# A deep-and-cross network kernel: the first superblock's transposing load and W1 change places on the SyncE queue

## The chip, the cores and the metric

The kernel runs on one core of a Trainium2 chip. The metric is device time in microseconds (us); a lower value is better. The kernel before was run eight times: 128.59, 128.99, 129.03, 129.17, 129.41, 128.19, 129.28 and 130.51 us, with a median of 129.1 us.

## The reference

```python
B, F, D, L = 4096, 26, 16, 6
Din = min(F * D, 1024)            # 416
# x0: (4096, 416), ws: (6, 416, 416), bs: (6, 416), all bfloat16

def reference(x0, ws, bs):
    x = x0
    for l in range(ws.shape[0]):
        x = x0 * (x @ ws[l] + bs[l]) + x
    return x
```

Each layer multiplies the 4096 x 416 activations by a 416 x 416 matrix, adds a bias, multiplies elementwise by the first input x0 and adds the activations of the layer before. Written out, x after layer l is x0 * (1 + the sum of x_j @ ws[j] + bs[j] over all layers j up to l). The kernel uses this form.

## The kernel before, in words

**Tiling.** The kernel works with transposed activations: features lie on the 128 partitions and batch rows run along the free dimension. The 416 features are three chunks of 128 (`NC = 3`, together `DF = 384`) and a rest of 32 (`DR`), called the tail. The 4096 rows are cut into `NS = 4` superblocks of `SB = 1024` rows, each of two halves of `H = 512` or four groups of `G = 256`. A step n is one layer of one superblock; there are 24, superblock after superblock and within it layer after layer (L308 to L421). The last one is done with rows on the partitions, ready for the store (L423 to L491).

**One step on TensorE (PE).** PSUM keeps the running sum over the layers, so nothing is added back by hand. A step consists of:

- `chunk(0..2, 0)`: 36 matmuls for half 0 (L255 by way of `tile_mm`, each 128 deep and 32 wide, four side by side). Each waits for the eviction of its input of the step before (`s_xa`, L341), and in superblock 0 the first waits for the layer's weights (`s_w[l]`, L360).
- the row matmuls, the part of the product that comes from the 32 tail features (L383 and L399). They use the small weights `wt_sb` and `wc_sb`. They wait for the tail of the step before (`s_sw`, L374) and for its last eviction (`s_xb`, L369); in step 0 for `x0t_sb` (`s_te`) and the small weights (`s_wt`, `s_wtp`, `s_wc`, L378 to L393). Their end is announced by `s_ti` (L410). VectorE (DVE) may then evict half 0, and SyncE waits for it before it issues later weights.
- 12 matmuls of 256 columns for the tail's 32 output features, for all four row groups (L415), announced by `s_to`.
- `chunk(0..2, 1)`: 36 matmuls for half 1 (L421), announced one chunk at a time by `s_mb`.

**The other engines.** DVE evicts six 128 x 512 tiles in each step, computing (PSUM + bias sum) * x0 (L527). The tail has a path of its own: ScalarE (ACT) reads it from PSUM (L585) after `s_to`, GpSimd (POOL) multiplies it by x0 (L232), and ACT copies it to neighbouring lanes (L556), which gives `s_sw` for the next step's row matmuls.

**The input of superblock 0.** Row blocks 0 to 5 (rows 0 to 767) are loaded as they lie into `xin_sb` (L135 to L137), are transposed by PE (L302, and L281 for blocks 4 and 5) and are copied into `x0T_sb` by DVE and ACT. The tail features of rows 768 to 1023 come in `xtl_sb` (L139). The 384 main features of rows 768 to 1023 come by a transposing load straight into `x0T_sb[:, :, 768:1024]` (L157, semaphore `s_x0T[0]`). PE waits for that in step 0 alone, at L412, after the row matmuls and before the tail matmuls, which are the first to read these rows, in their fourth group:

```python
ins.then_inc(s_ti, 1)                      # L410
if n == 0:
    pe.wait_ge(s_x0T[0], 16)               # L412
for k in range(NC):
    for g in range(4):
        ins = tile_mm(... src[:, k, off + g * G:off + (g + 1) * G], g, False)
```

**The queues around the change.** The SyncE queue (SP) issues by hand, in this order: the biases (L134), row blocks 0 and 1 (L135), row blocks 4 and 5 (L136), the transposing load L157, the main weights W1 of layer 1 (L163 with l = 1, 312 KB, `s_w[1]`), and four loads of the tail weights `wt_sb` of layers 1 to 5 (L125 through L165, `s_wt[1]`). Nothing among these waits. Then SP waits for `s_ti` before it issues W2 and the rest (L159). The ACT queue issues row blocks 2 and 3 (L137), W0 (L138), `xtl_sb` (L139) and two small `wt_sb` loads for layer 0 (L548, issued by L125, `s_wt[0]`). The POOL queue issues two `wt_sb` loads for layer 0 (`s_wtp`) and four `wc_sb` loads (L196), of which the first two are layer 0's (`s_wc[0]`).

Of the kernel before, what the change touches and what calls it, by code (L numbers as in the profile page):

```python
# [11 lines left out]
def bass_standalone__dcn_v2_cross__recsys_kernel(  # L12
# [9 lines left out]
    DF = 128 * NC  # L22
    DR = D - DF
    assert DR == 32
    SB = 1024
# [7 lines left out]
    with ExitStack() as es:  # L33
        def sb(name, shape, dt=BF16):
            return es.enter_context(nc.sbuf_tensor(name, shape, dt))
# [7 lines left out]
        x0T_sb = sb("x0T_sb", [128, NC, B])  # L43
# [20 lines left out]
        def sem(name):  # L64
            return es.enter_context(nc.semaphore(name))
# [8 lines left out]
        s_x0T = [sem("s_x0T%d" % i) for i in range(NS)]  # L74
# [16 lines left out]
        def wmain(l):  # L91
            return ws[l, 0:DF, :].rearrange("(k p) n -> p k n", p=128)
# [12 lines left out]
        def lane(g):  # L105
            return slice(32 * g, 32 * g + 32)
# [9 lines left out]
        def store(eng, a, n, by_pool):  # L116
            eng.wait_ge(s_o, a + n - by_pool)
            if by_pool:
                eng.wait_ge(s_oP, by_pool)
            assert a % 2 == 0 and n == 2  # L120
            eng.dma_start(out_w[:, (j0 + a) // 2, :, :], o_sb[:, j0 + a:j0 + a + n, :]).then_inc(s_out, 16)

        def load_wt(eng, g, a, b, done):
            n0, n1 = ((0, 256), (256, DF))[g % 2]
            eng.dma_start(  # L125
                wt_sb[lane(g), a:b, 0:n1 - n0], ws[a:b, DF:D, n0:n1].rearrange("l p n -> p l n")
            ).then_inc(done, 16)
# [19 lines left out]
        @block.sync  # L147
        def _(sp):
            def load_rows(s):
                sp.dma_start_transpose(  # L150
                    x4_sb[:, s - 1:s, :], x0[s * SB:(s + 1) * SB, D - 128:D]
                ).then_inc(s_x4[s - 1], 16)
                sp.dma_start_transpose(
                    x0T_sb[:, :, s * SB:(s + 1) * SB], x0[s * SB:(s + 1) * SB, 0:DF]
                ).then_inc(s_x0T[s], 16)

            sp.dma_start_transpose(x0T_sb[:, :, 768:SB], x0[768:SB, 0:DF]).then_inc(s_x0T[0], 16)  # L157
            for l in range(1, L):
                if l > 1:  # L159
                    sp.wait_ge(s_ti, (1, 2, 2, 2)[l - 2])  # L160
                if l == L - 1:
                    load_rows(1)
                sp.dma_start(w_sb[:, l, :, :], wmain(l)).then_inc(s_w[l], 16)  # L163
                if l == 1:
                    for g in range(4):  # L165
                        load_wt(sp, g, 1, L, s_wt[1])
            for s in range(NS - 1):
                n = (s + 1) * L
                sp.wait_ge(s_xa, NC * n)
                sp.wait_ge(s_xb, NC * n)  # L170
                for c in range(NC):
                    sp.dma_start_transpose(
                        o_sb[:, s * JS:(s + 1) * JS, c * 128:(c + 1) * 128], xo_sb[:, s, c, :]
                    ).then_inc(s_oT, 16)
                sp.wait_ge(s_xt, n)
                sp.dma_start_transpose(ot_sb[:, s, :, :], xot_sb[:, s, :]).then_inc(s_ot, 16)
                if s < NS - 2:
                    load_rows(s + 2)
                if s == 0:
                    for g in range(4):  # L180
                        sp.dma_start(wl_sb[lane(g), :], ws[L - 1, DF:D, :]).then_inc(s_wl, 16)
                if s == 1:
                    sp.dma_start(x0n_sb[:, :, :].rearrange("p (g r) d -> p g r d", r=2), x0_w[:, j0 // 2:, :, :]).then_inc(s_x0n, 16)
                sp.wait_ge(s_oT, 16 * NC * (s + 1))
                sp.wait_ge(s_otc, s + 1)
                sp.dma_start(
                    out_v[:, s * JS:(s + 1) * JS, :], o_sb[:, s * JS:(s + 1) * JS, :]
                ).then_inc(s_out, 16)
            store(sp, 0, 2, 0)
            store(sp, 4, 2, 2)  # L190
# [458 lines left out]
```

## Time and profile before

| what | value |
|---|---|
| median of 8 runs | 129.1 us |
| the profiled execution's own time | 128.59 us |
| its span, first to last instruction | 127.3 us |
| PE busy | 123.1 us, 97% of the span |
| DVE busy | 99.8 us, 78% |
| ACT busy | 67.6 us, 53% |
| POOL busy | 24.1 us, 19% |
| granted TensorE clock | 9 tenths or more in all 40 slices; 1.0 for the core |

The page of the profile describes one execution. PE is the engine of the matmuls and PEld is its weight load, which runs beside it. "Idle before" is the time an engine stood still ahead of an instruction, with the instruction or the transfer that ended the wait. For a DMA the profile gives the time of issue and the time from there to landing, when its semaphore is complete; "SPq", "ACTq" and "POOLq" are the queues of the engines that issue. All stage times below count from the start of the span.

### The profile page before, as it was taken

Reading aid. Unit: us, or ns where it says so; the run is one execution under the profiler, and the core shown is the slowest. Engines: PE = TensorE matmul, PEld = TensorE weight load, DVE = VectorE, ACT = ScalarE, POOL = GpSimd, SP = SyncE. Lnnn points to the kernel's source line nnn. Section 1 sums busy time; section 2 is a strip of 40 time slices with the busy share of each in tenths; the row PEclk is TensorE's granted clock in tenths of the full one; section 3 lists DMA queues with packets and bytes.
Section 4 is the critical chain, followed back from the end, with each engine's and each line's share of the span. In section 5 each row is a group of like instructions: output and inputs, shape, how many; then the busy total and the mean of one; then the engine's idle time right before and its main releaser. Section 6 shows DMA issues by size and latency. Waiting matters only on the chain.

```text
span 127.3 us, 5318 instructions
## 1 busy us (share of the span) xinstructions
PE 123.1 (97%) x2410; PEld 62.2 (49%) x2410; DVE 99.8 (78%) x154; ACT 67.6 (53%) x146; POOL 24.1 (19%) x44
## 2 busy tenths in 40 slices
PE   7799999999999999999999999999999999999991
PEld 5554444445445445445445445444444444454660
DVE  2339779779779789788797797797797797797973
ACT  0627357476735555574743563574762564566830
POOL 7512102102012023022022022022021020220450
PEclk9999999999999999999999999999999999999999
DMA  3983299400009969720006769960007820430006
GB/s 104 278 194 106 47 224 244 122 5 0 5 3 128 153 109 226 218 83 5 0 5 128 145 113 233 324 205 0 0 5 46 176 56 0 160 113 5 0 28 245
DMA packets 32577, 13.49 MB, mean 106 GB/s; under 512 B 24870, under 2 KB 32556, under 8 KB 32556
## 3 DMA queue, kind: packets, MB, share of 16 engines
q1 hardware_dynamic: 31036, 12.12, 45.0%
q10 hardware_dynamic: 1328, 0.99, 2.5%
q8 instruction: 19, 0.31, 1.1%
q0 software_dynamic: 192, 0.06, 0.2%
q14 instruction: 2, 0.02, 0.1%
HBM read 3.86 MB, written 3.41 MB: 57 GB/s over the span
## 4 chain that ended last, share of the span: by engine, by line
PE 94%; DMA 3%; DVE 0%; ACTq 0%; issue 0%
PE ps L255 81%; PE ps L383 10%; DMA w_sb<-in_ws_dram 3%; PE ps L439 2%; PE ps L454 1%; DVE o_sb L540 0%; PE ps L478 0%; ACTq L137 0%; PE ps L399 0%; PE ps L484 0%
## 5 line engine op out<-in xcount | busy, mean ns | idle before, releaser
L527 DVE SCALAR_TENSOR_TENSOR xT_sb<-ps,cb_sb,x0T_sb 128x512 bf16<-128x512 f32 x120 | 81.0, 743 | 16.4 <-PE ps L383 16.3
L255 PE MATMUL ps<-xT_sb,w_sb 128*32 128x512 bf16 (+1 forms) x1596 | 84.2, 364 | 0.0
L255 PEld LDWEIGHTS ps<-xT_sb,w_sb 128*32 128x32 bf16 x1596 | 40.9, 97 | 37.2 <-issue 4.0
L556 ACT ACTIVATE xt_sb<-xt_sb 32x256 bf16<-32x256 bf16 x76 | 31.5, 414 | 15.7 <-POOL xt_sb L232 15.1
L585 ACT ACTIVATE t_sb<-ps,cb_sb 64x256 f32<-64x256 f32 x46 | 21.6, 469 | 31.1 <-PE ps L255 30.8
L232 POOL TENSOR_TENSOR xt_sb<-t_sb,x0t_sb 128x256 bf16<-128x256 f32 x20 | 13.5, 673 | 81.4 <-ACT t_sb L585 81.4
L255 PE MATMUL ps<-x0T_sb,w_sb 128*32 128x512 bf16 (+1 forms) x336 | 18.5, 364 | 0.8 <-DMA w_sb<-in_ws_dram 0.8
L527 DVE SCALAR_TENSOR_TENSOR xo_sb<-ps,cb_sb,x0T_sb 128x512 bf16<-128x512 f32 x18 | 12.1, 744 | 2.5 <-PE ps L383 2.5
L255 PEld LDWEIGHTS ps<-x0T_sb,w_sb 128*32 128x32 bf16 x336 | 8.5, 97 | 8.3 <-DMA w_sb<-in_ws_dram 0.9
L383 PE MATMUL ps<-xt_sb,wt_sb 32*128 32x512 bf16 x76 | 11.5, 379 | 0.0
L604 ACT ACTIVATE x0t_sb<-x_sb 32x512 bf16<-32x512 bf16 x12 | 7.5, 626 | 0.3
L399 PE MATMUL ps<-xt_sb,wt_sb 32*128 32x512 bf16 x38 | 7.4, 385 | 0.0
L383 PE MATMUL ps<-xt_sb,wc_sb 32*128 32x256 bf16 x76 | 7.3, 268 | 0.0
L383 PEld LDWEIGHTS ps<-xt_sb,wt_sb 32*128 32x128 bf16 x76 | 2.2, 92 | 8.1 <-DVE xT_sb L527 8.1
L383 PEld LDWEIGHTS ps<-xt_sb,wc_sb 32*128 32x128 bf16 x76 | 3.8, 93 | 2.2
L232 POOL TENSOR_TENSOR xot_sb<-t_sb,x0t_sb 128x256 bf16<-128x256 f32 x3 | 2.0, 675 | 12.6 <-ACT t_sb L585 12.6
L540 DVE SCALAR_TENSOR_TENSOR o_sb<-ps,x0n_sb 128x416 bf16<-128x416 f32 x6 | 3.3, 586 | 1.0 <-PE ps L484 0.9
L560 ACT ACTIVATE xo_sb<-ps,cq_sb 128x512 bf16<-128x512 f32 x5 | 3.3, 685 | 1.1 <-PE ps L383 1.1
L551 ACT ACT_TABLE_LOAD x1 | 1.3, 1283 | 3.6 <-issue 3.6
L130 PE MATMUL ps<-const-bfloat16-1.0 128*32 128x256 bf16 x40 | 2.3, 418 | 0.8 <-PEq L634 0.8
L439 PE MATMUL ps<-w_sb,xT_sb 128*128 128x416 bf16 x12 | 2.8, 340 | 0.0
L507 DVE CAST x0T_sb<-ps 128x256 bf16<-128x256 f32 x2 | 0.8, 420 | 2.5 <-PE ps L255 2.5
(52 smaller groups left out, 41.2 us busy)
## 6 DMA issues: line engine op xcount, KB each, us to landing
out_dram<-o_sb SPq DMA_DIRECT2D x3, 832.0 KB, 4.8
w_sb<-in_ws_dram SPq DMA_DIRECT2D x5, 312.0 KB, 4.6
x0n_sb<-in_x_dram SPq DMA_DIRECT2D x1, 832.0 KB, 5.5
xin_sb<-in_x_dram SPq DMA_DIRECT2D x2, 208.0 KB, 3.7
out_dram<-o_sb SPq DMA_DIRECT2D x2, 208.0 KB, 2.0
out_dram<-o_sb ACTq DMA_DIRECT2D x2, 208.0 KB, 2.0
w_sb<-in_ws_dram ACTq DMA_DIRECT2D x1, 312.0 KB, 4.3
xin_sb<-in_x_dram ACTq DMA_DIRECT2D x1, 208.0 KB, 2.7
```

Source lines behind the costliest of these rows:

```text
L130: nc.tensor.matmul(ps[lane(q % 4), 7, 0:256], lhsT=CONST[:, 0:32], rhs=CONST, start=True, stop=True, skip_group_check=True, tile_position= ...
L232: pool.tensor_tensor(out=dst, in0=t32_sb[:, n % 2, :], in1=x0t_sb[:, s, 0:G], op=ALU.mult).then_inc(s_xt, 1)
L255: return pe.matmul(dst, lhsT=lhsT, rhs=rhs, start=start, stop=True, skip_group_check=True, tile_position=(0, 32 * q),)
L383: return pe.matmul(dst, lhsT=lhsT, rhs=srct[lane(g), cols], start=l == 0 and start, stop=True, skip_group_check=True, tile_position=(32 * ...
L399: pe.matmul(ps[:, NC * h + 2, :], lhsT=wt_sb[lane(g), l, 0:128], rhs=srct[lane(g), :].rearrange("p (b r) -> p b r", b=2)[:, ::-1, :], star ...
L439: pe.matmul(ps[:, NAT_BANKS[t], 0:D], lhsT=xT_sb[:, (L - 1) % 2, k, rows], rhs=w_sb[:, L - 1, k, :], start=False, stop=True, skip_group_ch ...
L527: dve.scalar_tensor_tensor(out=dst, in0=ps[:, NC * half + c, :], scalar=cb_sb[:, c, l:l + 1], in1=x0T_sb[:, c, o:o + H], op0=ALU.add, op1= ...
L540: dve.scalar_tensor_tensor(out=o_sb[:, j0 + t, :], in0=ps[:, NAT_BANKS[t], 0:D], scalar=1.0, in1=x0n_sb[:, t, :], op0=ALU.add, op1=ALU.mul ...
L556: ins = act.activation(out=buf[lane(g), G:2 * G], in_=buf[lane(g ^ 1), 0:G], func=ACTF.Copy)
L560: act.activation(out=xo_sb[:, NS - 1, c, half * H:(half + 1) * H], in_=ps[:, NC * half + c, :], func=ACTF.Identity, bias=cq_sb[:, c:c + 1] ...
L585: ins = act.activation(out=t32_sb[HALVES[h], n % 2, :], in_=tail(h), func=ACTF.Identity, bias=cb_sb[HALVES[h], NC, l:l + 1],)
L604: ins = act.activation(out=x0t_sb[lane(g), s + 1, :].rearrange("p (b n) -> p b n", b=2), in_=src[:, ::-1, :] if g % 2 else src, func=ACTF. ...
```

## The change

The transposing load of rows 768 to 1023 is issued after W1 rather than ahead of it, still ahead of the four `wt_sb` loads. No other instruction changes, on any engine. SP's list has the same 31 entries, two of them exchanged.

```diff
-            sp.dma_start_transpose(x0T_sb[:, :, 768:SB], x0[768:SB, 0:DF]).then_inc(s_x0T[0], 16)
             for l in range(1, L):
                 if l > 1:
                     sp.wait_ge(s_ti, (1, 2, 2, 2)[l - 2])
...
                 sp.dma_start(w_sb[:, l, :, :], wmain(l)).then_inc(s_w[l], 16)
                 if l == 1:
+                    sp.dma_start_transpose(x0T_sb[:, :, 768:SB], x0[768:SB, 0:DF]).then_inc(s_x0T[0], 16)
                     for g in range(4):
                         load_wt(sp, g, 1, L, s_wt[1])
```

## The prediction

> **What bounds the kernel now.** I read the page first, for the chain of work that ended last. It is PE from end to end, apart from the start:
>
> ```profile
> PE 94%; DMA 3%; DVE 0%; ACTq 0%; issue 0%
> PE ps L255 81%; PE ps L383 10%; DMA w_sb<-in_ws_dram 3%; PE ps L439 2%; PE ps L454 1%; DVE o_sb L540 0%; PE ps L478 0%; ACTq L137 0%; PE ps L399 0%; PE ps L484 0%
> ```
>
> Any microsecond by which PE is late in step 0 therefore counts, unless something behind it absorbs it. Next I read the table of waits in the first 9.5 us, for the transfers that anybody waits for:
>
> ```profile
> PEld ps L255 <- DMA w_sb<-in_ws_dram: 0.9, 1, 0.9
> PE ps L255 <- DMA w_sb<-in_ws_dram: 0.8, 1, 0.8
> PEld ps L383 <- DVE x0T_sb L507: 0.5, 1, 0.5
> PEld ps L255 <- DMA bsa_sb<-in_bs_dram: 0.4, 1, 0.4
> PEld ps L255 <- issue: 0.2, 1, 0.2
> ```
>
> The transfers waited for are the biases and one weight load, W0, whose wait ends at 5.60. No row names the transposing load, W1 or the small weights. The two loads that change places are both hidden today, so the question is how well. The timeline gives the issues (start, duration, engine, line), and the list of DMA issues, asked for narrow windows, the landings (last column: us from issue to landing):
>
> ```profile
> 2.21 1.28 SPq L157 DMA_TRANSPOSE x0T_sb<-in_x_dram  x1
> 2.33 1.21 ACTq L125 DMA_DIRECT2D wt_sb<-in_ws_dram  x2
> 3.55 0.58 SPq L163 DMA_DIRECT2D w_sb<-in_ws_dram  x1
> 4.16 1.92 SPq L125 DMA_DIRECT2D wt_sb<-in_ws_dram  x4
> ```
>
> ```profile
> x0T_sb<-in_x_dram SPq DMA_TRANSPOSE x1, 5.4
> w_sb<-in_ws_dram SPq DMA_DIRECT2D x1, 312.0 KB, 4.8
> wt_sb<-in_ws_dram ACTq DMA_DIRECT2D x1, 8.0 KB, 5.0
> ```
>
> The transposing load lands at 2.21 + 5.4 = 7.6, W1 at 3.55 + 4.8 = 8.3, and the later of ACT's two small loads (issued at 2.85) at 7.85. Who reads them, and when, is in PE's weight-load timeline, with ACT's tail copies beside it:
>
> ```profile
> 8.27 0.09 PEld L383 LDWEIGHTS ps<-x0t_sb,wt_sb 32*128 32x128 bf16 x1 [0.47 <-DVE x0T_sb L507]
> 8.57 0.09 PEld L383 LDWEIGHTS ps<-x0t_sb,wc_sb 32*128 32x128 bf16 x1
> 8.90 1.96 PEld L255 LDWEIGHTS ps<-x0T_sb,w_sb 128*32 128x32 bf16 x48 [0.21 <-issue]
> 10.97 1.83 PEld L255 LDWEIGHTS ps<-xT_sb,w_sb 128*32 128x32 bf16 x36
> 13.22 0.09 PEld L383 LDWEIGHTS ps<-xt_sb,wt_sb 32*128 32x128 bf16 x1 [0.42 <-DVE xT_sb L527]
> ...
> 11.27 1.69 ACT L556 ACTIVATE xt_sb<-xt_sb 32x256 bf16<-32x256 bf16 x4 [0.79 <-POOL xt_sb L232]
> ```
>
> The wait of L412 stands ahead of the group at 8.90. So the transposing load has 8.90 - 7.6 = 1.3 us to spare. W1's first reader starts at 10.97, so W1 has 10.97 - 8.3 = 2.7 us. ACT's small weights, read at 8.27, have 0.4 us, and POOL's wc_sb (second load issued at 3.33, 4.8 us to landing, 8.1), read at 8.57, have 0.5 us.
>
> **W1 comes earlier.** It is issued at 2.21 and may land about 1.3 us sooner. Nobody waited for it, so this is worth 0.
>
> **The transposing load comes later.** Its issue moves by W1's own issue time, 0.58 us, to 2.79. If issue alone set its landing, it would land at 8.2. That is the lower bound. But the engines have work at that time: the table by windows shows 325 and 344 GB/s from 3 to 5 us, and a DMA share near or over 1 up to 8 us, so a load's landing is set by the bytes ahead of it. W1 is 312 KB, 319,488 bytes. At the mean of these two rates, 335 GB/s, it takes 0.95 us; at the 207 GB/s of the stretch from 5 to 6, the lowest there, 1.54 us. The landing is then 7.6 + 0.95 = 8.55, or 9.15 as the upper bound of this working. I take 8.55, because W1 itself ran in such a stretch (241 and 300 GB/s from 6 to 8 us) and landed only 0.7 us after the transposing load. 8.55 lies ahead of 8.90, so PE is not held.
>
> **If it is late after all,** not every bit of it counts. When PE starts its tail matmuls d later, DVE is not held: it evicts half 0 from 9.12 for 2 us anyway, while half 1's first chunk, 24 matmuls after 8.90, is there by about 10.2 (84 matmuls take 4.33 us in the chain), and is needed at 11.1. What shifts by d is the tail path (ACT L585, POOL L232, ACT L556), which ends at 11.27 + 1.69 = 12.96. The next row matmuls start at 13.22, held by DVE's last eviction; PE's own weight loads were through at 12.80, the idle 0.42 before 13.22. So 0.26 us is absorbed and the rest passes 1:1 to the end. The landing that decides is 8.90 + 0.26 = 9.16. Even the bound of 9.15 costs nothing that shows.
>
> **The loads that now stand beside others.** SP's four wt_sb loads (L125) keep their place behind both, with the same bytes ahead of them; their first reader is the row group at 13.22, against a last landing near 10. SP's next wait is for s_ti; it was through with its issues at 6.1 and waits until 9.0. The small loads of ACT and POOL are the delicate ones: they meet W1 where they met the transposing load. [...] The row says 5.0 us from issue to landing for 8 KB, landing 0.25 us behind the transposing load that SP began to issue 0.64 us earlier. As measured, it stood behind SP's work. If it now stood behind both SP loads, it would land at 7.85 + 0.95 = 8.8, the row matmuls of 8.27 would be 0.53 us late, and nothing absorbs that, since DVE's evictions wait for them (0.67 us before 9.12). I take a value between, from the order of issue: the transposing load would now begin at 2.79, only 0.06 us ahead of this small load. ACT's first small load stands like that today (2.33, against 2.21) and lands after 4.8 us, at 7.1, 0.5 ahead of the transposing load. The second would then land at 8.55 - 0.5 = 8.05, under 8.27: cost 0, with both ends, 0 and 0.53, kept. POOL's second wc_sb load by the same upper end would land at 9.05 against 8.57, 0.48 late, in the same stall and not added to it.
>
> **Could it gain?** PE's start at 5.61 hangs on W0 (ACT queue, issued 1.27). If W1's packets disturbed W0 less than the transposing ones, the start could move up, but not ahead of ACT's second input copy by much: that ends at 5.52 and the second third of the matmuls needs it. Also xtl_sb lands only at 1.79 + 4.8 = 6.6, and its transposes start at 6.91. So the gain is below 0.3 us.
>
> The sum is 0 us in the likely case, against the profiled execution's own 128.59 us (span 127.3 and 1.3 around it). The runs' median lies 0.5 us above that execution, and I set the difference on the median: 129.1 + 0.0 = 129.1 us. Against a measurement, 0.5% (0.65 us) is about what can be told from no change.
>
> **Rivals.**
> 1. The small weights become the wait. Mechanism: ACT's and POOL's small loads fall behind both SP loads. For it speaks the 5.0 us for 8 KB, against it the order of issue. Price 0.53 us: 129.6 us. It decides from a landing of 8.27.
> 2. The slower one: the transposing load does not stream behind W1 but runs after it, and the wait of L412 becomes real. [...] the nearest row, W2 issued alone at 9.02, landed after 2.9 us. Taken as a full serial cost, by the row, the landing is 7.6 + 2.9 = 10.5, which is 10.5 - 9.16 = 1.3 us too late: 130.4 us. For it speaks that the transposing load of superblock 1 (L153) took 8.0 us to land, 3.6 after its 4.4 us of issue. Against it: W1 landed 0.7 us behind the transposing load, so these loads overlap. It decides from a landing of 9.16.
> 3. The change takes effect and nothing follows, because both stay hidden: the forecast.
> 4. W0 gains the 0.3 us: 128.8 us, which counts as no change too.
>
> **How the numbers follow.** Forecast 0.60 (129.1); small weights late 0.16 (129.6, mostly within 0.5%, 0.03 of it beyond); serial transposing load 0.14 (130.4); W0 earlier 0.06; a gain over 0.65 us that I cannot name 0.04. Faster 0.05, same 0.78, slower 0.17. The runs before scatter from 128.2 to 130.5, so their median is uncertain by a few tenths. The range starts at 128.6 and ends at 130.1, past the small-weights case at 129.6 and its higher price (a full 1.54 for W1: 7.85 + 1.54 - 8.27 = 1.1, 130.2), without the serial case's full price. The likeliest case's own range is 128.8 to 129.5.
>
> **What would show it.** Right: in the profile after, the group at 8.90 has "issue" ahead of it and not a DMA, the transposing load lands between 8.2 and 9.15, W1 near 7, and the steps from 13.2 on have the same times. The small-weights case would show as a DMA wait ahead of L383 near 8.3, the serial one as a wait for x0T_sb ahead of L255 after 9. The prediction is wrong if the landing passes 9.16 or if W0's wait moves by more than 0.3 us.

## The result and the profile after

The changed kernel's median is 129.3 us (20 runs), against 128.55 us for the kernel before (57 runs, the eight shown earlier among them). The ratio is 1.0051, with a 95% interval of 1.0032 to 1.0070, so the change costs about 0.65 us. The ratio leaves out the few executions of a slower state that both kernels fall into now and then. A second series gave 1.0054 (1.0033 to 1.0075). No change was forecast; the kernel became slower, and the prediction was wrong. That 129.3 lies only 0.2 us from the forecast 129.1 is luck: the median of the first eight runs, on which the forecast stood, was 0.55 us above that of all 57.

The profiled execution after took 128.84 us with a span of 127.6. Its chain of waits has a new link:

```profile
PE 91%; DMA 4%; ACTq 2%; DVE 0%; issue 0%
PE ps L255 79%; PE ps L383 10%; DMA wt_sb<-in_ws_dram 4%; PE ps L439 2%; PE ps L454 1%; DVE o_sb L540 0%; ACTq L139 0%; ACTq L138 0%; ACTq L125 0%; PE ps L478 0%; ACTq L137 0%; PE ps L399 0%; PE ps L484 0%
```

Where W0 stood (w_sb, 3%), there is now a load of the small tail weights (wt_sb, 4%) with ACT's queue behind it. The table of waits up to 9.8 us says the same:

```profile
PEld ps L383 <- DVE x0T_sb L507: 1.2, 1, 1.2
...
PE ps L383 <- DMA wt_sb<-in_ws_dram: 0.7, 1, 0.7
...
PEld ps L255 <- DMA w_sb<-in_ws_dram: 0.3, 1, 0.3
```

Before, the row matmuls (L383) waited for DVE's input copy alone; now PE waits another 0.7 us, for wt_sb. The weight load's 1.2 us, put down to DVE, is the same wait: DVE's copy had ended at 8.09. The issues and the landings of the two exchanged loads and of ACT's second small load:

```profile
2.22 0.47 SPq L162 DMA_DIRECT2D w_sb<-in_ws_dram  x1
2.32 0.96 ACTq L125 DMA_DIRECT2D wt_sb<-in_ws_dram  x2
2.73 1.28 SPq L164 DMA_TRANSPOSE x0T_sb<-in_x_dram  x1
```

```profile
w_sb<-in_ws_dram SPq DMA_DIRECT2D x1, 312.0 KB, 5.0
...
x0T_sb<-in_x_dram SPq DMA_TRANSPOSE x1, 6.1
...
wt_sb<-in_ws_dram ACTq DMA_DIRECT2D x1, 8.0 KB, 5.5
```

W1 lands at 7.3, the transposing load at 2.73 + 6.1 = 8.8, the small load (issued at 2.84) at 8.4. Their readers in the timeline:

```profile
8.59 0.09 PEld L383 LDWEIGHTS ps<-x0t_sb,wt_sb 32*128 32x128 bf16 x1 [1.15 <-DVE x0T_sb L507]
8.62 0.37 PE L383 MATMUL ps<-x0t_sb,wt_sb 32*128 32x512 bf16 x1 [0.69 <-DMA wt_sb<-in_ws_dram]
...
9.16 1.96 PEld L255 LDWEIGHTS ps<-x0T_sb,w_sb 128*32 128x32 bf16 x48 [0.21 <-issue]
...
13.49 0.09 PEld L383 LDWEIGHTS ps<-xt_sb,wt_sb 32*128 32x128 bf16 x1 [0.42 <-DVE xT_sb L527]
```

From 13.49 on every step has its old length; the whole loss lies in step 0. The profiles bear this out: time less the start of step 1's row matmuls is 115.3 or 115.4 us in all thirteen profiled executions of this document but e1's (128.59 - 13.22 before, 128.84 - 13.49 after). This execution was among the faster ones of the changed kernel. Another one (e10_after_third, 129.66 us) has all three late loads as gates, one after the other:

```profile
8.95 0.09 PEld L383 LDWEIGHTS ps<-x0t_sb,wt_sb 32*128 32x128 bf16 x1 [1.49 <-DVE x0T_sb L507]
9.43 0.09 PEld L383 LDWEIGHTS ps<-x0t_sb,wt_sb 32*128 32x128 bf16 x1 [0.35 <-issue]
9.89 1.96 PEld L255 LDWEIGHTS ps<-x0T_sb,w_sb 128*32 128x32 bf16 x48 [0.32 <-DMA x0T_sb<-in_x_dram]
14.22 0.09 PEld L383 LDWEIGHTS ps<-xt_sb,wt_sb 32*128 32x128 bf16 x1 [0.42 <-DVE xT_sb L527]
```

against a second profiled execution of the kernel before (e9_before_again, 128.16 us):

```profile
7.91 0.09 PEld L383 LDWEIGHTS ps<-x0t_sb,wt_sb 32*128 32x128 bf16 x1 [0.59 <-DVE x0T_sb L507]
8.48 1.96 PEld L255 LDWEIGHTS ps<-x0T_sb,w_sb 128*32 128x32 bf16 x48 [0.21 <-issue]
12.81 0.09 PEld L383 LDWEIGHTS ps<-xt_sb,wt_sb 32*128 32x128 bf16 x1 [0.42 <-DVE xT_sb L527]
```

In e10 ACT's second small load landed at 8.73, POOL's second wc_sb load at 9.32 and the transposing load at 9.85, each followed by the row that reads it. Step 1's row matmuls come 1.41 us later than in e9; the two times differ by 1.50.

The loads in all profiled executions with these two orders of the queue, in us. A landing is the moment when the load's semaphore is complete (issue plus the list's last column; here with the trace's second decimal). The packet columns come from the trace's packet records: ACT's small loads are the 64 packets of 256 bytes on ACT's queue, the transposing load is the first 768 such packets on SP's. The kernel of e12, told below, has the changed order and differs in what PE waits for.

| kernel | W0 lands | ACT's small loads: last packet ends | second one lands | POOL's second wc_sb load lands | transposing load: first packet | lands |
|---|---|---|---|---|---|---|
| before | 5.56 | 6.67 | 7.84 | 8.09 | 5.00 | 7.60 |
| e9, before again | 4.87 | 6.37 | 7.69 | 7.91 | 5.01 | 7.43 |
| after | 4.94 | 6.46 | 8.38 | 8.59 | 6.03 | 8.82 |
| e5, after again | 4.98 | 7.05 | 9.08 | 9.43 | 6.04 | 9.87 |
| e10, after, third | 4.94 | 6.93 | 8.73 | 9.32 | 6.08 | 9.85 |
| e12, changed order | 5.29 | 6.48 | 7.87 | 8.45 | 5.86 | 8.82 |

The packets of ACT's small loads are through at 6.4 to 7.1 in both kernels, before PE wants the weights. What is late is the landing: it follows the last packet by 1.2 and 1.3 us in the kernel before, and by 1.4 to 2.0 in the changed order.

### The profile page after: what moved, and what is told of

The parts are those of the page before. It is cut to its first block, busy times and chain, and to the rows that moved or that the text cites. A ratio compares the mean times of both kernels' runs of the same rounds, so it can differ in the third digit from the quotient of the medians.

```text
span 127.6 us, 5318 instructions
## 1 busy us (share of the span) xinstructions
PE 123.4 (97%) x2410; PEld 62.5 (49%) x2410; DVE 99.9 (78%) x154; ACT 67.6 (53%) x146; POOL 24.1 (19%) x44
## 2 busy tenths in 40 slices
DMA packets 32577, 13.49 MB, mean 106 GB/s; under 512 B 24870, under 2 KB 32556, under 8 KB 32556
## 4 chain that ended last, share of the span: by engine, by line
PE 91%; DMA 4%; ACTq 2%; DVE 0%; issue 0%
PE ps L255 79%; PE ps L383 10%; DMA wt_sb<-in_ws_dram 4%; PE ps L439 2%; PE ps L454 1%; DVE o_sb L540 0%; ACTq L139 0%; ACTq L138 0%; ACTq L125 0%; PE ps L478 0%; ACTq L137 0%; PE ps L399 0%; PE ps L484 0%
## 5 line engine op out<-in xcount | busy, mean ns | idle before, releaser
L255 PE MATMUL ps<-xT_sb,w_sb 128*32 128x512 bf16 (+1 forms) x1596 | 84.2, 364 | 0.0
L255 PEld LDWEIGHTS ps<-xT_sb,w_sb 128*32 128x32 bf16 x1596 | 40.9, 97 | 37.2 <-issue 4.0
L255 PE MATMUL ps<-x0T_sb,w_sb 128*32 128x512 bf16 (+1 forms) x336 | 18.6, 366 | 0.1
L255 PEld LDWEIGHTS ps<-x0T_sb,w_sb 128*32 128x32 bf16 x336 | 8.6, 97 | 7.8 <-issue 1.0
L383 PE MATMUL ps<-xt_sb,wt_sb 32*128 32x512 bf16 x76 | 11.5, 379 | 0.0
L383 PE MATMUL ps<-xt_sb,wc_sb 32*128 32x256 bf16 x76 | 7.3, 268 | 0.0
L383 PEld LDWEIGHTS ps<-xt_sb,wt_sb 32*128 32x128 bf16 x76 | 2.2, 92 | 8.1 <-DVE xT_sb L527 8.1
L383 PEld LDWEIGHTS ps<-xt_sb,wc_sb 32*128 32x128 bf16 x76 | 3.8, 93 | 2.2
L383 PE MATMUL ps<-x0t_sb,wt_sb 32*128 32x512 bf16 x16 | 2.4, 378 | 0.7 <-DMA wt_sb<-in_ws_dram 0.7
```

The costliest lines, as they stand in the source:

```text
L255: return pe.matmul(dst, lhsT=lhsT, rhs=rhs, start=start, stop=True, skip_group_check=True, tile_position=(0, 32 * q),)
L383: return pe.matmul(dst, lhsT=lhsT, rhs=srct[lane(g), cols], start=l == 0 and start, stop=True, skip_group_check=True, tile_position=(32 * ...
```

## The experiments

Theory: step 0's small weights, which ACT and POOL load, land late because they share the fate of the transposing load, which is now behind W1; their wait is the loss. Rival: the transposing load's own wait (L412) is the loss. Third: W1's traffic delays W0 and PE's start. Line numbers shift by a few with the edits: L257, for example, is L255 in another kernel.

**e1_w1_on_act.** W1 ahead of the small loads, but on ACT, with the transposing load where it was.

```diff
         nc.scalar.dma_start(xtl_sb[:, :, :], x0_v[:, 6:JS, DF:D]).then_inc(s_xtl0, 16)
+        nc.scalar.dma_start(w_sb[:, 1, :, :], wmain(1)).then_inc(s_w[1], 16)
...
-                sp.dma_start(w_sb[:, l, :, :], wmain(l)).then_inc(s_w[l], 16)
+                if l > 1:
+                    sp.dma_start(w_sb[:, l, :, :], wmain(l)).then_inc(s_w[l], 16)
```

> W1 is issued by ACT between xtl_sb and ACT's two small wt_sb loads; the transposing load is issued on SP where it was before the change, so it is not behind W1 in its queue, but the small loads are. Small-weights theory (the row matmuls of step 0 wait for small weights that land behind W1): slower than the kernel before by 0.4 to 1.0 us (about 129.2 from 128.55), a DMA wait ahead of L383, small weights landing at 8.3 or later, although the transposing load lands near 7.6. Transposing-load theory (the wait of L412 is what costs): the same as before, 128.55 within 0.25 us, no DMA wait ahead of L383. W0 theory (W1's traffic disturbs PE's start): PE's start later than 5.6.

Ratio 1.0189 (1.0127 to 1.0250), some 2.4 us, far above the 0.4 to 1.0 expected; it rests on three executions (130.52, 130.90 and 131.92). The profiled one had a granted clock of 0.987, so only the order of landings is read from it. The wait, and the landings of the transposing load (issued at 2.21) and of ACT's second small load (issued at 3.62):

```profile
PE ps L385 <- DMA wt_sb<-in_ws_dram: 2.5, 1, 2.5
```

```profile
x0T_sb<-in_x_dram SPq DMA_TRANSPOSE x1, 7.7
...
wt_sb<-in_ws_dram ACTq DMA_DIRECT2D x1, 8.0 KB, 7.3
```

The small load, behind both, lands at 10.9 and holds PE, as the theory has it. Against the expectation, the transposing load, issued ahead of W1 in time, is late as well (9.9), so this run does not separate the two theories. The edit did something else too: ACT, busy issuing W1, began its own work at 4.25 instead of 3.57, and PE's matmuls stood 0.4 us for ACT's input copy (L553).

**e2_small_ahead.** The changed kernel with the small loads ahead of W1: ACT's two go to SP, and POOL's first two wc_sb loads to ACT.

```diff
+            for g in (1, 3):
+                load_wt(sp, g, 0, 1, s_wt[0])
...
-            for i in range(2):
-                for g in (1, 3):
-                    load_wc(i, g)
+            for g in (1, 3):
+                load_wc(1, g)
...
+            act.wait_ge(s_zero, 1)
             for g in (1, 3):
-                load_wt(act, g, 0, 1, s_wt[0])
+                act.dma_start(
+                    wc_sb[lane(g), 0:1, 32 * g:32 * g + 32], ws[0:1, DF:D, DF:D].rearrange("l p n -> p l n")
+                ).then_inc(s_wc[0], 16)
```

> The changed kernel, but step 0's small weights stand ahead of W1: ACT's two wt_sb loads go to SP between row blocks 4-5 and W1, and POOL's first two wc_sb loads go to ACT in their place. The transposing load is then still behind W1 and is issued 0.9 us later than in the changed kernel. Small-weights theory: the row matmuls are not held any more (L383 follows DVE's cast by 0.2 us or less), and the time falls back to 128.6 to 128.8. Transposing-load theory: stays at 129.2 or more, with a DMA wait ahead of L255 at about 9.

Ratio 1.0001 (0.9982 to 1.0019): the loss is gone, although the transposing load is still behind W1. Small loads landed by 7.5, the transposing load at 8.5:

```profile
8.70 0.09 PEld L384 LDWEIGHTS ps<-x0t_sb,wt_sb 32*128 32x128 bf16 x1 [0.47 <-DVE x0T_sb L508]
9.33 1.96 PEld L256 LDWEIGHTS ps<-x0T_sb,w_sb 128*32 128x32 bf16 x48 [0.21 <-issue]
```

Neither row has a DMA ahead of it. That the row matmuls are as late as 8.70 has another cause, told in the last section. The small weights (7.5) would have been in time for e9's 7.91 as well; the transposing load, landing at 8.54, would just have been late for e9's 8.48. It also lands earlier here than in the changed kernel (8.82 to 9.87), so this run alone does not part the two waits; e12 does.

**e3_third_ahead.** 104 KB of W1 ahead instead of 312 KB.

```diff
-                sp.dma_start(w_sb[:, l, :, :], wmain(l)).then_inc(s_w[l], 16)
+                if l == 1:
+                    sp.dma_start(w_sb[:, 1, 0, :], ws[1, 0:128, :]).then_inc(s_w[1], 16)
+                else:
+                    sp.dma_start(w_sb[:, l, :, :], wmain(l)).then_inc(s_w[l], 16)
                 if l == 1:
                     sp.dma_start_transpose(x0T_sb[:, :, 768:SB], x0[768:SB, 0:DF]).then_inc(s_x0T[0], 16)
+                    sp.dma_start(w_sb[:, 1, 1:NC, :], wmain(1)[:, 1:NC, :]).then_inc(s_w[1], 16)
...
-                            pe.wait_ge(s_w[l], 16)
+                            pe.wait_ge(s_w[l], 32 if l == 1 else 16)
```

> Only the first third of W1 (104 KB) goes ahead of the transposing load, the other two thirds follow it. Small-weights theory: the small weights land about a third as late as in the changed kernel (0.3 us less slack than before, of 0.4), so a loss of 0 to 0.25 us: 128.55 to 128.8. Transposing-load theory: its landing moves by 0.3 to 0.4 us and nothing is lost, 128.55. A fixed cost per load put ahead (not bytes) would leave most of the 0.65 us.

Ratio 1.0017 (0.9994 to 1.0041), no loss that can be told from zero. The small load lands at 7.70, the transposing load at 8.21. This speaks for a cost that grows with the bytes put ahead and against a fixed cost per load, which would have left most of the 0.65 us; the interval reaches 0.5 us, so it is not excluded.

**e4_w1_w2_ahead.** 624 KB ahead.

```diff
-                sp.dma_start(w_sb[:, l, :, :], wmain(l)).then_inc(s_w[l], 16)
+                if l != 2:
+                    sp.dma_start(w_sb[:, l, :, :], wmain(l)).then_inc(s_w[l], 16)
                 if l == 1:
+                    sp.dma_start(w_sb[:, 2, :, :], wmain(2)).then_inc(s_w[2], 16)
                     sp.dma_start_transpose(x0T_sb[:, :, 768:SB], x0[768:SB, 0:DF]).then_inc(s_x0T[0], 16)
```

> W1 and W2 (624 KB) go ahead of the transposing load; W2 is not held for s_ti. Small-weights theory: ACT's small loads were issued between W1 and the transposing load in time; if they stand behind W2 too, L383 is late by a further 0.9 us and the time is about 130.2; if they stand ahead of W2 (issue order), L383 stays as in the changed kernel and the transposing load, landing near 9.7, holds L255 by 0.5 to 0.8 us: 129.6. Transposing-load theory: landing near 9.7, L383 not held by a DMA, L255 held, 129.8 to 130.2.

Ratio 1.0126 (1.0086 to 1.0165), 1.6 us, more than the branch that fits its landings had (129.6). The transposing load lands at 10.40 and is waited for; POOL's second wc_sb load (9.26) and xtl_sb (7.50) were waits too, so the total is not one load's. The small load, issued at 2.84 ahead of the transposing load (3.27), lands at 7.98, 0.6 us after its last packet, where the changed order has 1.4 to 2.0. This hints that the place beside the transposing load, more than the bytes of W1, makes it late.

**e5_after_again.** The changed kernel, unedited.

> The changed kernel once more, for the size of the loss and a second profile. Small-weights theory: again 0.4 to 0.8 us over the kernel before, the start of the row matmuls of step 0 (L383) again set by a DMA wait for small weights, landing after 8.3, whether PE started early or late. If in this profile L383 follows DVE's cast without such a wait, or L255 waits for the transposing load, the theory holds only for the first profile.

Ratio 1.0054 (1.0033 to 1.0075). L383 stood until 9.37 for wt_sb (1.1 us), and L415's group until 9.94, just after the transposing load's landing at 9.87. The two waits nearly coincide.

**e6_act_small_ahead.** Of e2's edit only one half: ACT's two loads are put on SP ahead of W1, and POOL's stay.

> The changed kernel with ACT's two wt_sb loads alone put on SP ahead of W1; POOL's wt_sb and wc_sb loads stay as they are. If ACT's loads alone cost the time: back to the kernel before within 0.2 us, no DMA wait at L383. If POOL's wc_sb loads (8.59 in the changed kernel's profile, read 0.3 us after the first row matmul) are the next gate: a wait for wc_sb remains and 0.2 to 0.5 us of the loss stay. The transposing load lands near 8.9 and must not be waited for under the small-weights theory.

Ratio 1.0018 (0.9999 to 1.0036): about two thirds of the loss goes with ACT's two 8 KB loads, and the rest can't be told from zero. POOL's second wc_sb load landed at 7.6 without having been moved; the transposing load is issued behind it here (3.65, it at 3.33). In the profile PE waits for the transposing load, which was not to be under the theory:

```profile
7.88 0.09 PEld L385 LDWEIGHTS ps<-x0t_sb,wt_sb 32*128 32x128 bf16 x1 [0.45 <-DVE x0T_sb L509]
8.96 1.96 PEld L257 LDWEIGHTS ps<-x0T_sb,w_sb 128*32 128x32 bf16 x48 [0.65 <-DMA x0T_sb<-in_x_dram]
13.29 0.09 PEld L385 LDWEIGHTS ps<-xt_sb,wt_sb 32*128 32x128 bf16 x1 [0.42 <-issue]
```

**e7_before_small_ahead.** e2's small loads in the kernel before, ahead of the transposing load: a candidate for beating both kernels.

> The kernel before (transposing load ahead of W1) with step 0's small weights ahead of both on SP and ACT, as in e2_small_ahead. In the kernel before they land 0.4 us ahead of their reader, so they cost nothing in the profile; if in other executions PE comes to them earlier, they may. Expected 128.4 to 128.7, the same as before or up to 0.2 us faster.

Ratio 1.0010 (0.9992 to 1.0028): no gain. With 7.2 to 7.4 for the small weights nothing waits for them, but nothing waited before either.

**e8_transposing_load_last.** W1, the four wt_sb loads, then the transposing load.

```diff
                 if l == 1:
-                    sp.dma_start_transpose(x0T_sb[:, :, 768:SB], x0[768:SB, 0:DF]).then_inc(s_x0T[0], 16)
                     for g in range(4):
                         load_wt(sp, g, 1, L, s_wt[1])
+                    sp.dma_start_transpose(x0T_sb[:, :, 768:SB], x0[768:SB, 0:DF]).then_inc(s_x0T[0], 16)
```

> W1, then SP's four wt_sb loads (240 KB), then the transposing load, which lands about 0.7 us later than in the changed kernel, near 9.5. Does a late transposing load pass 1:1 to the end, or are 0.26 us absorbed as the prediction had it? With the group at L415 due 0.57 us after the first row matmul's weight load: 1:1 theory: the next step's row matmuls come later by all of the wait; absorption theory: by the wait less 0.26 us. Small-weights theory for the total: the same loss at L383 or less (the small loads now have W1 and some of the wt_sb loads ahead), plus the L415 wait: 129.2 to 129.9.

Ratio 1.0120 (1.0078 to 1.0162), above the range expected. ACT's second small load, issued at 2.84 as ever, and the transposing load, issued at 4.71:

```profile
wt_sb<-in_ws_dram ACTq DMA_DIRECT2D x1, 8.0 KB, 4.4
```

```profile
x0T_sb<-in_x_dram SPq DMA_TRANSPOSE x1, 5.3
```

The small load lands at 7.3, with W1 ahead of it and 80 KB of wt_sb issued beside it: earlier than in the kernel before. It lands 0.6 us after its last packet, as in e4. In this one execution W1 alone does not make it late, which points at the transposing load beside it. And the transposing load is now the wait:

```profile
8.68 0.09 PEld L383 LDWEIGHTS ps<-x0t_sb,wt_sb 32*128 32x128 bf16 x1 [0.47 <-DVE x0T_sb L507]
...
10.05 1.96 PEld L255 LDWEIGHTS ps<-x0T_sb,w_sb 128*32 128x32 bf16 x48 [0.87 <-DMA x0T_sb<-in_x_dram]
14.37 0.09 PEld L383 LDWEIGHTS ps<-xt_sb,wt_sb 32*128 32x128 bf16 x1 [0.42 <-issue]
```

**e9_before_again, e10_after_third, e11_small_ahead_again.** One profiled execution each, of the kernel before, the changed one and e2.

> The kernel before, one more look, for the scatter of its landings. Both theories: L383 follows DVE's cast by 0.6 us with no DMA wait; ACT's second small load lands at 7.6 to 8.1, the transposing load at 7.4 to 7.9, W1 after it. If the landings of the kernel before scatter as widely as those of the changed kernel (8.8 and 9.9 for the transposing load), the difference between the two is partly chance.

> The changed kernel, a third look. If the small loads share the fate of the transposing load they are issued beside: they land 0.4 to 0.8 us ahead of it, at 8.2 or later, and L383 waits for them; the transposing load lands at 8.7 to 9.9 and is due at about the same time, so that each of the two waits hides the other.

> Small weights ahead of W1 and of the transposing load, a second look. Small loads land by 7.5 and are not waited for; the transposing load, although issued 0.9 us later than in the changed kernel, lands at 8.4 to 9.0. If it lands near 9.9 here too, the recovery of this kernel is not due to the small weights alone.

e9 and e10 are in the table above: in two executions of the kernel before the three late landings differ by at most 0.2 us, in four of the changed order by 1.0 to 1.2, and each one's earliest is later than the latest of the kernel before (for ACT's load by 0.03 us only). e11 has the small wt_sb load at 7.30, but ACT's wc_sb load at 8.07, later than the 7.5 expected and still in time, and the transposing load at 9.06, which L256 waited for until 9.17, about when it was due.

**e12_rows_not_waited.** The changed kernel with the wait of L412 taken away; step 0 computes with other rows in place of the late ones.

```diff
-                        o = off + half * H
+                        o = off + half * (256 if n == 0 else H)
...
-                    if n == 0:
-                        pe.wait_ge(s_x0T[0], 16)
...
-                                src[:, k, off + g * G:off + (g + 1) * G], g, False,
+                                src[:, k, off + (g - (n == 0 and g == 3)) * G:off + (g - (n == 0 and g == 3) + 1) * G], g, False,
...
+                        elif n == 0:
+                            dve.wait_ge(s_x0T[0], 16)
```

> The changed kernel, but step 0 doesn't read the rows of the transposing load on PE: its fourth tail group and its half 1 read columns 512 to 767 and 256 to 767 of x0T_sb instead, and the wait for the transposing load stands on DVE ahead of half 1's evictions, at about 11. The work is the same, the values of these rows are not. What is left of the loss is then the small weights' alone. Small-weights theory as first stated (they are the whole loss): 0.4 to 0.7 us over the kernel before. If the two waits overlap, as in the third look at the changed kernel (row matmuls held to 8.95 and 9.43, the group at L415 to 9.89): 0.2 to 0.1 us less than the changed kernel's loss, so 0.4 to 0.6 us. If the transposing load is the larger part: under 0.25 us.

Ratio 1.0046 (1.0028 to 1.0064). Most of the loss, 0.6 of some 0.7 us, is there without any wait of PE for the transposing load; the interval (0.4 to 0.8 us) leaves room for all of it. Its profile is of the fastest of these executions (128.59 us), and there POOL's wc_sb load (8.45), not ACT's (7.87), is what PE stands for, 0.2 us beyond the 0.28 between the same two rows in e6:

```profile
8.09 0.09 PEld L383 LDWEIGHTS ps<-x0t_sb,wt_sb 32*128 32x128 bf16 x1 [0.48 <-DVE x0T_sb L505]
8.56 0.09 PEld L383 LDWEIGHTS ps<-x0t_sb,wt_sb 32*128 32x128 bf16 x1 [0.34 <-DVE x0T_sb L505]
8.91 1.96 PEld L255 LDWEIGHTS ps<-x0T_sb,w_sb 128*32 128x32 bf16 x48 [0.21 <-issue]
```

With e2 (1.0001) and e6 (1.0018) from the other side, the small weights' wait, ACT's and POOL's, is shown as the main loss. The transposing load's own wait mostly hides behind it (0.0 to 0.1 us in after, e5 and e10); the 0.2% that e6 has left fits it, but is not clear of zero.

## Why the prediction was wrong, point by point

- **What bounds the kernel; W1's worth.** Right. PE carries the chain, and W1's earlier landing (7.3 to 8.0 against 8.2 and 8.3, first read after 11) gained nothing.
- **The transposing load's landing.** Taken as 8.55, with 9.15 as the upper bound. Measured 8.82, 9.87 and 9.85. The term of 0.95 us for W1's 319,488 bytes, an estimate from the 335 GB/s of before, was too small for the landing: against 7.60 and 7.43 before, W1 ahead costs 1.2 us at the least and 2.4 at the most. It was right for the start, for the first transposing packet moved by about 1 us, from 5.0 to between 5.9 and 6.1. The rest came after that: the packets take 1.4 to 2.1 us from first to last (1.3 and 1.6 before), and the landing follows the last by 1.4 to 1.8 (1.0 and 1.1). The table by windows of e10, then of e9 (PEclk, DMA share and GB/s are the last three columns):

```profile
6.00:7.00 1.00, 1.00 (x37) 0.50 (x29) 0.00 (x0) 0.00 (x0) 0.00 (x0) 1.00 2.10 222
7.00:8.00 1.00, 0.95 (x47) 0.46 (x34) 0.66 (x2) 0.76 (x2) 0.06 (x1) 1.00 0.57 110
```

```profile
6.00:7.00 1.00, 1.00 (x43) 0.73 (x39) 0.00 (x0) 0.00 (x0) 0.00 (x0) 1.00 1.17 282
7.00:8.00 1.00, 0.88 (x40) 0.41 (x28) 0.75 (x2) 0.87 (x2) 0.19 (x1) 1.00 1.18 259
```

In e10 the packets of 6 to 7 us take so long that their sum passes the window twice (a DMA share of 2.10), and from 7 to 8 the engines move 110 GB/s, with work outstanding.
- **The small weights.** This is the step that failed: "The second would then land at 8.55 - 0.5 = 8.05, under 8.27: cost 0". The load landed at 8.38, 9.08 and 8.73 and held PE (7.87 in e12, where POOL's held it). The sum counts the bytes ahead of the load; what made it late is the time from its last packet, at 6.5 to 7.1, to its landing (1.4 to 2.0 us, against 1.2 and 1.3 before). That it lands ahead of the transposing load held (by 0.4, 0.8 and 1.1 us), but the landing from which this was counted was too early. And 8.27, the reader's time, came from an execution in which W0 landed at 5.56. In the others W0 landed at 4.9 to 5.3, and e9's PE was at the row matmuls at 7.91, with the small weights there at 7.69: 0.2 us to spare, not 0.4. By the same token the 0.3 us set as the most that W0 could gain were too few: e9's row matmuls are 0.36 us earlier. Of the ends of 0 and 0.53 us the runs passed the upper one, 0.65. POOL's wc_sb load, "in the same stall and not added to it", made a stall of 0.2 us of its own in e12.
- **The row of 5.0 us for 8 KB.** The lower end, cost 0, left ACT's small load at the 7.85 of before; that it would stay there was the author's estimate. Its packets were hardly later: the last one ends at 6.5 to 7.1 in the changed order, against 6.4 and 6.7 before. The landing was (8.38 to 9.08 in the changed kernel), and for that the row, 5.0 us from issue to landing, was the better guide. What ties a small load's landing to the transposing load is not shown: the gap from last packet to landing is 0.6 us in e8 and e4, where the transposing load is issued later, and 1.2 to 2.0 beside it.
- **The 0.26 us absorbed.** Wrong. In the kernel before, step 1's row matmuls follow DVE's first eviction by 4.10 us (13.22 - 9.12), and the group at L415 precedes it by 0.22. In e6 (DVE at 8.74) the group is 0.44 late and the rows 13.29 - 8.74 - 4.10 = 0.45; in e8 (9.61) 0.66 and 0.66; in e4 (9.94) 0.72 and 0.72. Nothing is absorbed: PE's 84 matmuls take their 4.33 us from the group at L415 on and PE is busy throughout (a share of 1.00 in each window from 9 to 13 us in the kernel before), so its weight loads' idle 0.42, there in these rows too, is no slack. The landing that decides was 8.90, not 9.16.
- **Rivals.** The first happened, with 0.65 us for its 0.53; the second in part, 1.2 to 2.4 us of delay where a full serial 2.9 was priced. W0 did not gain (5.56 and 4.87 before, 4.94 to 4.98 after). The range's end of 130.1 was called "past" the small weights' higher price, which the same sentence puts at 130.2.
- **Left open.** Why the transposing load stalls longer behind W1. In the trace's packet records the transposing packets nearly cease while the last few 832-byte packets of W1 go out: of the sixteen 4-byte packets at W1's end in e10, fifteen are out by 6.84 and the last at 7.48. Per 0.2 us: 832-byte packets on SP's queue (plain loads), its 256-byte packets (the transposing load; from 7.8 on later loads too), and the mean ns of the latter:

```text
e10 (after), from us   6.0  6.2  6.4  6.6  6.8  7.0  7.2  7.4  7.6
832-byte packets        47   16   19    8    5    6    5    2    0
256-byte packets        37  136  168   93   39   23    8    9  123
mean ns of these        18   18   44  142   94   41   60   18   23

e9 (before), from us   5.0  5.2  5.4  5.6  5.8
832-byte packets         9    5    0    0    0
256-byte packets        55  169  194  108  180
mean ns of these        18   18   22   30   21
```

In e4 the transposing packets all but stop from 8.0 to 8.6, when the last 832-byte packet is through. The last such packet starts at 6.70 in after, 6.62 in e12, 7.31 in e5, 7.44 in e10 and 8.61 in e4, and the transposing load lands at 8.82, 8.82, 9.87, 9.85 and 10.40. In e5 and e10 SP's issue of it was longer too, 1.79 and 1.83 us against 1.28 in after. A later last packet goes with a later landing in these five, but for 0.02 us between e5 and e10; that one sets the other is not shown, and what holds up the last packets of W1 was not tried.

## What to carry to other kernels

Before a large load is moved ahead in a queue, list every transfer issued in the same microsecond on every queue, with its slack to its reader. Here the smallest and most urgent loads paid, not only the one that was exchanged, and putting them ahead of W1 took the loss away (e2, 1.0001). Count to the landing, not to the last packet: 8 KB whose packets were through at 6.5 landed at 8.4. Take the slack from several executions, since a reader held by something else in one profile looks safer than it is. Bytes over bandwidth, 0.95 us, gave the start of the transposing load behind W1 (about 1 us later), not its landing (1.2 to 2.4 us later).

## What the hardware showed beyond that

Some executions run PE's first matmuls at about half the later rate, while the granted clock in the table by windows stands at 1.00 (e2, 5 to 8 us). e2's weight loads, four matmuls of 128x512 at a time:

```profile
5.63 0.18 PEld L256 LDWEIGHTS ps<-x0T_sb,w_sb 128*32 128x32 bf16 x4 [0.25 <-issue]
6.05 0.18 PEld L256 LDWEIGHTS ps<-x0T_sb,w_sb 128*32 128x32 bf16 x4 [0.25 <-issue]
6.48 0.18 PEld L256 LDWEIGHTS ps<-x0T_sb,w_sb 128*32 128x32 bf16 x4 [0.25 <-issue]
```

A group of four comes every 0.42 us, where in step 1 of the kernel before nine such groups take 1.83 us, 0.20 each. The slow stretch ends at 6.0 in e5 and at 6.8 to 7.1 in e2, e11, e7 and e8, and is not seen in e6, e9 and e10, where these matmuls start at 5.1 to 5.2. PE reaches the row matmuls at 8.70 in e2, at 7.91 in e9; 0.1 us of this is a later start. What sets its end is not shown. Two executions of the changed kernel, e5 and e10, differ in it, so the edits need not be its cause; that it is chance in e2, where both profiles have it, is not shown. It is why single profiles of these kernels are not compared by their times: 0.8 us is more than the change.
